# Attention values of two heads side by side in 64-column tiles, with summed exponentials for the denominators

## The chip, the cores and the metric

The kernel runs on one core of a Trainium2 chip. The metric is the device time of one execution in microseconds (us). Before the change three executions took 840.5, 841.15 and 843.84 us (median 841.15). The engines are TensorE (PE; its weight loads are shown apart as PEld), VectorE (DVE), ScalarE (ACT), GpSimd (POOL) and the DMA queues that SyncE (SP) and POOL issue.

## The reference

An attention in which a query sees only the keys of its own hash bucket, then two feed-forward blocks. All is float32.

```python
# q, k, v: (2, 8, 768, 64); proj: (64, 6)
q_bucket = sum over bits of ((q @ proj) > 0) * 2**bit      # k_bucket the same
scores = where(q_bucket == k_bucket, (q @ k.T) / 8, -1e9)
attn = exp(scores - max(scores))
attn = attn / (sum(attn) + 1e-9)
x = (attn @ v)  as (1536, 512)
g = x @ w_gate; h1 = (g * sigmoid(g) * (x @ w_val)) @ w_out                  # d_ff 1536
h = h1 @ w_in;  out = (max(h, 0) + alpha * min(h, 0)) @ w_out2              # d_ff 2048
```

## The kernel before

**Items and units.** The attention is cut into 24 items: a batch, a pair of heads and a group of 256 queries. Each item has two units, one a head (`u.x` is 0 or 1). A unit's scores lie transposed, with 768 keys as six blocks of 128 partitions and 256 queries along the free axis. A unit goes through four parts:

- `banks`: three steps, each of which multiplies keys and queries for two key blocks into a PSUM tile `S` (`s_bank`, lines 307 and 308); ACT copies it into `se` (128 x 1536 for the six blocks, four buffers) and DVE starts the maximum (`s_max`).
- `top` and `back`: the maximum over keys by TensorE transposes (`s_mt`, `s_mb`) and a DVE reduction, then `s_sub`, one DVE operation over all of `se` (line 344). ACT takes the exponential in place (`s_exp`, line 350), released a little later by `release()`.
- `values`: three steps of two key blocks (`s_pv`, line 361). The stationary operand is a 128 x 128 slice of `vv`. `vv` holds head 0's 64 value columns, 64 columns of ones and head 1's 64 value columns, so one matmul of 128 stationary columns gives a head's 64 output rows and, in the other 64 rows, its denominators. Six matmuls a unit, twelve an item, all plain float32.
- After the second unit `s_den` copies the denominators out of `po` with two ACT operations (line 367), `s_out` makes the reciprocals with two DVE transposes (lines 377 to 379) and multiplies each head by them (line 383, two operations), and `s_xh`, `s_xl` split the result into two float32r parts for the next stage.

**Order.** Units are written one slot apart: part k of unit i belongs to slot i + k. Items 0 to 7 run alone. Items 8 to 15 are written between the steps of `stage1(0)`, and items 16 to 23 between those of `stage1(1)`; `stage1(c)` is the first feed-forward block (lines 756 to 758) for 512 tokens, and for each of its steps 1.9 attention steps are written. Stage 1 of the first tokens also brings in the weights: DMA, four integer operations on ACT, DVE and POOL (lines 616 to 621), and a split in two parts (lines 691 and 705). Then come `stage1(2)`, `stage2(1)` and two calls of `wino` without attention. When the kernel is built, a planner orders the instructions of each engine from the written order, the dependences and its own costs; each engine then works strictly in its order, save that TensorE loads weights ahead.

**Buffers.** `gh` and `gl` hold the gated activations of `stage1` in `NG1` buffers; a `quad` (four output banks) reads four of them at once.

Of the kernel before, what the change touches and what calls it, by code (L numbers as in the profile page):

```python
# [8 lines left out]
F32 = mybir.dt.float32  # L9
# [3 lines left out]
AF = mybir.ActivationFunctionType  # L13
ALU = mybir.AluOpType
# [3 lines left out]

BIG = float(2.0 ** 100)

NG1 = 5
NEX = (2, 3)
RAWB = 2
WB = (3, 4, 6)
# [24 lines left out]
EARLY = (0, 12)  # L49

AHEAD = 6

SUMS = (12, 14, 16, 17)

# [2 lines left out]
def lsh_attention_moe_kernel(  # L57
# [12 lines left out]
    nc = tc.nc  # L70
    B, H, D, S = qT.shape
# [3 lines left out]
    P = 128  # L75
    NC = S // P
    GQ = 256
    NG = S // GQ
    NPAIR = H // 2
# [4 lines left out]
    W = 512  # L84
# [53 lines left out]
    at = Bag()  # L138
# [210 lines left out]
    def s_exp(u):  # L349
        ins = nc.scalar.activation(out=u.se, in_=u.se, func=AF.Exp, scale=SCALE)  # L350
        at.exps.append(ins.ins.name)
        if not at.alone:
            tc.keep_in_program_order(ins)

    def s_pv(u, j):
        it = u.it
        if j == 0 and u.x == 0:
            tag = at.tag["po"][it.i % 2]
            it.po = at.ps.tile([P, 2, GQ], F32, tag=tag, name="po", bufs=at.nb[tag])
        for kb in (2 * j, 2 * j + 1):  # L360
            nc.tensor.matmul(it.po[:, u.x, :], lhsT=VV[it.b, it.p][:, kb, u.x * D:u.x * D + P], rhs=u.se[:, kb, :],  # L361
                             start=kb == 0, stop=kb == NC - 1)

    def s_den(it):
        it.den = at.sm.tile([P, 8, 32], F32, tag="den", name="den", bufs=1)
        for x in range(2):
            nc.scalar.activation(out=it.den[x * D:(x + 1) * D],
                                 in_=it.po[(1 - x) * D:(2 - x) * D, x, :].rearrange("p (a b) -> p a b", a=8),
                                 func=AF.Copy, bias=1e-9)

    def s_out(it):

        it.xf = at.sm.tile([P, GQ], F32, tag="xf", name="xf", bufs=1)
        dt_ = it.xf.rearrange("p (a b) -> p a b", a=8)
        rc = it.den
        r8 = at.sm.tile([P, 8, 1], F32, tag="r8", name="r8", bufs=1)
        nc.vector.transpose(out=dt_, in_=it.den)
        nc.vector.reciprocal(out=r8, in_=dt_[:, :, 0:1])
        nc.vector.transpose(out=rc, in_=r8.to_broadcast([P, 8, 32]))
        rf = rc.rearrange("p a b -> p (a b)")  # L380
        for x in range(2):
            r = slice(x * D, (x + 1) * D)
            nc.vector.tensor_tensor(out=it.xf[r], in0=it.po[r, x, :], in1=rf[r], op=ALU.mult)
# [9 lines left out]
    items = []  # L393
    for b in range(B):
        two = W // GQ
        order = [(p, g) for p in range(NPAIR) for g in range(two)] if b == 0 else []
        order += [(p, g) for g in range(two if b == 0 else 0, NG) for p in range(NPAIR)]
        for p, g in order:
            it = Bag()
            it.b, it.p, it.g, it.i = b, p, g, len(items)  # L400
            it.ready = False
            it.first = not any((o.b, o.p) == (b, p) for o in items)
            items.append(it)
    at.done = 0
# [4 lines left out]
    def attention():  # L409

        us = []
        for it in items:
            for x in range(2):
                u = Bag()
# [30 lines left out]
        held, last = [], []  # L445

        def release():
            while held:
                s_exp(held.pop(0))

        def give():
            while last:
                it = last.pop(0)
                s_xh(it)
                s_xl(it)
# [21 lines left out]
        def back(u):  # L477
# [5 lines left out]
            step()  # L483
            yield

        def values(u):
            for j in range(3):
                s_pv(u, j)
                if j == 2 and u.x == 1:
                    s_den(u.it)  # L490
                    s_out(u.it)
                    last.append(u.it)
                    if at.alone:
                        give()
                if EXP_AT == ("v", j):
                    release()
                if XH_AT == ("v", j):
                    give()
                step()
                yield  # L500

        order = []
        for i, u in enumerate(us):
            for k, part in enumerate((banks, top, back, values)):
                slot = i + LAGS[k]
                order.append(((slot, i, k) if slot < OLDER else (slot, k, i), part, u))
        order.sort(key=lambda o: o[0])
        for _, part, u in order:
# [450 lines left out]
    def g_tiles():  # L959
        return [at.lt.tile([P, W], F32R, tag=t, name=t, bufs=NG1) for t in ("gh", "gl")]  # L960

# [16 lines left out]
    VV = {}  # L978

    at.nb = dict(S=3, T=1, G=2, Y=1, po=1)  # L980
    at.tag = dict(mt="G", mb="G", hp="T", po=("Y", "po"), gates="G")
    at.gates = 0
    pr = wp.tile([P, 2, 44], F32, tag="wr", name="pr", bufs=2)
    nc.scalar.dma_start(out=pr, in_=proj)
    first_load(items[0])
# [3 lines left out]
    def more():  # L989

        if next(side, 0) == 0:
            kv.close()
            return False
        return True
# [9 lines left out]
            upto("load", min(i + RAWB, 7), w_load)  # L1004

    k = 0
    per = NPAIR * (W // GQ)
    while at.done < per:
        at.alone = at.done < per - 2
        more()  # L1010
# [8 lines left out]
    for c, rate in enumerate(RATES):  # L1019
# [4 lines left out]
        for _ in stage1(c):  # L1024
# [7 lines left out]
            while due >= 1.0:  # L1032
                due -= 1.0
                over += at.done >= per * (c + 2)
                if over <= AHEAD:
                    more()
# [90 lines left out]
```

## Time and profile before

| | |
|---|---|
| three executions | 840.5, 841.15, 843.84 us |
| the profiled execution's own time | 839.15 us |
| its span | 836.9 us |
| PE, PEld busy | 807.8 us (97%), 690.2 us (82%) |
| DVE, ACT, POOL busy | 588.7 us (70%), 489.3 us (58%), 313.5 us (37%) |
| granted TensorE clock, mean | 0.998 |

The span is measured from the first instruction to the last. A PE record's length holds its latency, and records overlap, so what one matmul costs is read from the distance of starts and not from its length. A plain float32 matmul leaves two records in the trace, a float32r matmul one.

### The profile page before, as it was taken

The numbers are of one execution on the slowest core, as the hardware profiler recorded it, in microseconds if no ns is written. First come the engines' busy times: TensorE is split into PE (matmuls) and PEld (weight loads), VectorE is DVE, ScalarE is ACT, GpSimd is POOL, SyncE is SP. The second block draws the span as 40 slices with busy tenths as digits, with TensorE's granted clock in tenths as the row PEclk, the third lists the DMA queues.
The fourth block names the chain that finished last, engine by engine and source line by source line (L and its number), as shares of the span: only waits on it lengthen the run. The fifth ranks groups of instructions, "written<-read, shape, count | busy, mean of one in ns | idle before, by whom it ended". The sixth has DMA issues, their size and how long they took to land.

```text
span 836.9 us, 12164 instructions
## 1 busy us (share of the span) xinstructions
PE 807.8 (97%) x4276; PEld 690.2 (82%) x4276; DVE 588.7 (70%) x905; ACT 489.3 (58%) x827; POOL 313.5 (37%) x253
## 2 busy tenths in 40 slices
PE   5998999999999999999999999999999999999998
PEld 4777878887878888888888888887788899989996
DVE  5889998887998866666664363567968575667553
ACT  7889877886766655555543232324655464555553
POOL 5133337666555633322221462442424311332220
PEclk9999999999999999999999999999999999999999
DMA  9322336877656538545444687878644477565554
GB/s 239 78 70 94 133 110 199 261 230 220 229 189 235 202 129 323 204 156 184 176 159 157 242 290 292 299 273 300 252 196 157 176 242 277 176 204 198 175 175 142
DMA packets 74475, 168.22 MB, mean 201 GB/s; under 512 B 18480, under 2 KB 36912, under 8 KB 73648
## 3 DMA queue, kind: packets, MB, share of 16 engines
q1 hardware_dynamic: 73264, 164.66, 57.3%
q0 software_dynamic: 1008, 2.75, 1.6%
q8 instruction: 34, 0.56, 0.3%
q14 instruction: 25, 0.20, 0.1%
q10 hardware_dynamic: 144, 0.05, 0.0%
HBM read 124.44 MB, written 42.99 MB: 200 GB/s over the span
## 4 chain that ended last, share of the span: by engine, by line
PE 71%; DVE 11%; ACT 7%; DMA 6%; issue 3%; POOL 1%; SPq 0%; DVEq 0%; ACTq 0%; POOLq 0%
PE po L361 10%; PE gp L756 8%; PE gp L758 8%; PE gp L757 8%; PE op L762 5%; PE op L761 5%; PE op L763 5%; DMA raw<-in_wblk_dram 5%; PE hp L757 5%; PE hp L758 5%; PE hp L756 4%; PE S L307 2%; PE S L308 2%; ACT se L309 2%; DVE wt L619 2%
## 5 line engine op out<-in xcount | busy, mean ns | idle before, releaser
L751 POOL TENSOR_TENSOR gl<-ex,gh 128x512 fp32r<-128x512 f32 x61 | 87.2, 1430 | 160.6 <-ACT gh L748 112.6
L361 PE MATMUL po<-se,vv 128*128 128x256 f32 x576 | 139.4, 381 | 5.1 <-ACT se L350 2.8
L361 PEld LDWEIGHTS po<-se,vv 128*128 128x128 f32 x576 | 106.4, 190 | 22.5 <-ACT se L350 4.6
L756 PE MATMUL gp<-xh,wb 128*128 128x512 f32 x288 | 120.1, 417 | 0.5 <-ACT xh L386 0.5
L758 PE MATMUL gp<-xh,wb 128*128 128x512 f32 x288 | 112.9, 392 | 0.0
L757 PE MATMUL gp<-xl,wb 128*128 128x512 f32 x288 | 112.6, 391 | 0.0
L748 ACT ACTIVATE gh<-ex 128x512 fp32r<-128x512 f32 x84 | 52.9, 630 | 74.4 <-DVE ex L745 47.1
L309 ACT ACTIVATE se<-S 128x512 f32<-128x512 f32 x144 | 81.8, 592 | 23.7 <-PE S L308 22.6
L621 POOL TENSOR_TENSOR wt<-wt,wr 128x512 int32<-128x512 int32 x48 | 63.1, 1319 | 86.5 <-DVE wt L619 39.7
L307 PE MATMUL S<-QA,kt 128*128 128x256 f32 x288 | 79.8, 304 | 6.8 <-ACT se L309 3.0
L344 DVE SCALAR_TENSOR_TENSOR se<-se,mb 128x1536 f32<-128x1536 f32 x48 | 83.6, 1741 | 3.4 <-PE mb L339 3.4
L350 ACT ACTIVATE se<-se 128x1536 f32<-128x1536 f32 x48 | 71.1, 1482 | 8.8 <-DVE se L344 8.6
L762 PE MATMUL op<-wb,gh 128*128 128x512 f32 x192 | 75.2, 392 | 0.9 <-DVE wb L705 0.9
L761 PE MATMUL op<-wb,gh 128*128 128x512 f32 x192 | 75.1, 391 | 0.0
L308 PE MATMUL S<-qb,kt 76*128 76x256 f32 x288 | 73.9, 286 | 0.9 <-ACT kt L221 0.5
L763 PE MATMUL op<-wb,gl 128*128 128x512 f32 x192 | 74.7, 389 | 0.0
L307 PEld LDWEIGHTS S<-QA,kt 128*128 128x128 f32 x288 | 54.8, 191 | 13.1 <-ACT se L309 4.7
L758 PEld LDWEIGHTS gp<-xh,wb 128*128 128x128 f32 x288 | 54.0, 188 | 11.9
L756 PEld LDWEIGHTS gp<-xh,wb 128*128 128x128 f32 x288 | 54.2, 188 | 10.1 <-ACT xh L386 1.0
L757 PEld LDWEIGHTS gp<-xl,wb 128*128 128x128 f32 x288 | 54.3, 189 | 9.1
L756 PE MATMUL gp<-gh,wb 128*128 128x512 f32 x144 | 61.3, 425 | 0.3 <-ACT gh L748 0.3
L308 PEld LDWEIGHTS S<-qb,kt 76*128 76x128 f32 x288 | 54.4, 190 | 4.0 <-ACT kt L221 0.8
(125 smaller groups left out, 1901.2 us busy)
## 6 DMA issues: line engine op xcount, KB each, us to landing
wb<-w SPq DMA_DIRECT2D x72, 512.0 KB, 3.8
raw<-in_wblk_dram SPq DMA_DIRECT2D x68, 512.0 KB, 4.4
wb<-s SPq DMA_DIRECT2D x48, 512.0 KB, 3.6
w<-wb SPq DMA_DIRECT2D x36, 512.0 KB, 3.0
s<-wb SPq DMA_DIRECT2D x24, 512.0 KB, 2.8
qr<-in_q_dram SPq DMA_DIRECT2D x24, 256.0 KB, 3.0
wb<-s SPq DMA_DIRECT2D x16, 256.0 KB, 3.7
nat<-in_k_dram SPq DMA_DIRECT2D x8, 384.0 KB, 3.6
```

What stands on the lines that cost most here:

```text
L307: nc.tensor.matmul(pt[:, i, :], lhsT=ka[:, sl], rhs=qa, start=True, stop=False)
L308: nc.tensor.matmul(pt[:, i, :], lhsT=kb[:, sl], rhs=qb, start=False, stop=True)
L309: nc.scalar.activation(out=u.se[:, 2 * j:2 * j + 2, :], in_=pt, func=AF.Copy)
L344: ins = nc.vector.scalar_tensor_tensor(out=u.se, in0=u.se, scalar=FLOOR, in1=u.mx[:, None, :].to_broadcast([P, NC, GQ]), op0=ALU.max, op1= ...
L361: nc.tensor.matmul(it.po[:, u.x, :], lhsT=VV[it.b, it.p][:, kb, u.x * D:u.x * D + P], rhs=u.se[:, kb, :], start=kb == 0, stop=kb == NC - 1)
L751: eng.tensor_tensor(out=l, in0=ex, in1=f32(h), op=ALU.subtract)
L756: nc.tensor.matmul(pt, lhsT=h, rhs=ah, start=first, stop=False)
L757: nc.tensor.matmul(pt, lhsT=h, rhs=al_, start=False, stop=False)
L758: nc.tensor.matmul(pt, lhsT=l, rhs=ah, start=False, stop=last)
L761: nc.tensor.matmul(pt, lhsT=gh, rhs=h, start=first, stop=False)
L762: nc.tensor.matmul(pt, lhsT=gh, rhs=l, start=False, stop=False)
L763: nc.tensor.matmul(pt, lhsT=gl, rhs=h, start=False, stop=last)
```

## The change

Items 8 to 23 (`it.pair`) multiply their values after both heads' exponentials are there. `s_pair` writes, for each key block, two matmuls of 64 stationary columns, one for each head, into the lower and the upper 64 rows of the same PSUM tile. The denominators come from other matmuls: `s_add` adds the exponentials of a unit over key blocks, and a 64-column block of ones is multiplied with the sums. In items 8 to 15 the sums are two 128 x 512 additions (DVE, then POOL), which leave two blocks a head and so four denominator matmuls an item; in items 16 to 23 there are three additions on DVE (two of 128 x 512, one of 128 x 256), which leave one block and two matmuls. The denominators then lie in the same rows as the values, so `s_den` and the multiplication of `s_out` are one operation each. The first unit's `values` steps become `rests`, three steps without matmuls, and the second's become `pair`, written first in the slot after. `ps` takes two buffers of 2 KB a partition; `gh` and `gl` go from five buffers to four.

```diff
-NG1 = 5
+NG1 = 4
...
+PAIRED = 8
+
+ADDS = ("DP", "DDD")
+
+RELEASE = 1
...
+    def s_add(u):
+
+        u.ps = at.sm.tile([P, 2, GQ], F32, tag="ps", name="ps", bufs=2)
+        how = ADDS[u.it.i // per - 1]
+        e = [dict(P=nc.gpsimd, D=nc.vector)[x] for x in how]
+        e[0].tensor_tensor(out=u.ps, in0=u.se[:, 0:2, :], in1=u.se[:, 2:4, :], op=ALU.add)
+        e[1].tensor_tensor(out=u.ps, in0=u.ps, in1=u.se[:, 4:6, :], op=ALU.add)
+        u.n = 4 - len(how)
+        if u.n == 1:
+            e[2].tensor_tensor(out=u.ps[:, 0, :], in0=u.ps[:, 0, :], in1=u.ps[:, 1, :], op=ALU.add)
+
+    def s_pair(it, ua, ub):
+
+        tag = at.tag["po"][it.i % 2]
+        it.po = at.ps.tile([P, 2, GQ], F32, tag=tag, name="po", bufs=at.nb[tag])
+        v = VV[it.b, it.p]
+        for k in range(NC):
+            for u in (ua, ub):
+                nc.tensor.matmul(it.po[u.x * D:(u.x + 1) * D, 0, :], lhsT=v[:, k, 2 * u.x * D:(2 * u.x + 1) * D],
+                                 rhs=u.se[:, k, :], start=k == 0, stop=k == NC - 1)
+        for k in range(ua.n):
+            for u in (ua, ub):
+                nc.tensor.matmul(it.po[u.x * D:(u.x + 1) * D, 1, :], lhsT=v[:, 0, D:2 * D],
+                                 rhs=u.ps[:, k, :], start=k == 0, stop=k == ua.n - 1)
+
     def s_den(it):
         it.den = at.sm.tile([P, 8, 32], F32, tag="den", name="den", bufs=1)
+        if it.pair:
+            nc.scalar.activation(out=it.den, in_=it.po[:, 1, :].rearrange("p (a b) -> p a b", a=8),
+                                 func=AF.Copy, bias=1e-9)
+            return
...
+        if it.pair:
+            nc.vector.tensor_tensor(out=it.xf, in0=it.po[:, 0, :], in1=rf, op=ALU.mult)
+            return
...
         def release():
             while held:
-                s_exp(held.pop(0))
+                u = held.pop(0)
+                s_exp(u)
+                if u.it.pair:
+                    s_add(u)
...
+        def rests(u):
+            for j in range(3):
+                if j == RELEASE:
+                    release()
+                step()
+                yield
+
+        def pair(u):
+            release()
+            for j in range(3):
+                if j == 0:
+                    s_pair(u.it, us[2 * u.it.i], u)
+                    s_den(u.it)
+                    s_out(u.it)
+                    last.append(u.it)
+                if j == 2:
+                    give()
+                step()
+                yield
...
+                if part is values and u.it.pair:
+                    order.append(((slot, -1, i), pair, u) if u.x else ((slot, k, i), rests, u))
+                    continue
```

The first place is TensorE at item 8, the first one changed (`po` is the values' PSUM tile, `hp` the hash of a later item, `gp` stage 1). Before, the first unit's six stand in twos, of which two runs are seen here:

```order
L758 MATMUL gp<-xh,wb 128x512
L361 MATMUL po<-se,vv 128x256 x2
L209 MATMUL hp<-QA,sqm 44x256
L210 MATMUL hp<-qb_67,sq_65 44x256
L209 MATMUL hp<-QA,sqm 44x256
L210 MATMUL hp<-qb_67,sq_65 44x256
L361 MATMUL po<-se,vv 128x256 x2
L756 MATMUL gp<-xh,wb 128x512
```

Now one matmul of the first head stands by itself, among stage 1 and the same hash:

```order
L823 MATMUL gp<-xh,wb 128x512
L821 MATMUL gp<-xh,wb 128x512
L215 MATMUL hp<-QA,sqm 44x256
L388 MATMUL po<-se,vv 64x256
L822 MATMUL gp<-xl,wb 128x512
L823 MATMUL gp<-xh,wb 128x512
```

and the other eleven with the four on `ps` come 29 matmuls later in one run:

```order
L821 MATMUL gp<-xh,wb 128x512
L822 MATMUL gp<-xl,wb 128x512
L823 MATMUL gp<-xh,wb 128x512
L388 MATMUL po<-se,vv 64x256 x11
L392 MATMUL po<-ps,vv 64x256 x4
L821 MATMUL gp<-xh,wb 128x512
L822 MATMUL gp<-xl,wb 128x512
L823 MATMUL gp<-xh,wb 128x512
```

The item's values moved from short runs for each unit into one matmul and one run of fifteen. The same split (one, then eleven) stands in 15 of the 16 changed items; in the last one all twelve are together.

The second place is DVE in the second half of the attention, around the additions into `acc` of stage 1 (`m` is the maximum, `se` the scores, `ex` a gate). Before:

```order
L315 TENSOR_TENSOR m_3258<-S,se 128x512
L793 TENSOR_TENSOR acc<-gp,acc 128x512
L317 SCALAR_TENSOR_TENSOR m_3258<-S,m_3258 128x512
L344 SCALAR_TENSOR_TENSOR se<-se,mb 128x1536
L331 TENSOR_TENSOR m_3258<-m_3258 128x256
L793 TENSOR_TENSOR acc<-gp,acc 128x512
L742 SCALAR_TENSOR_TENSOR ex<-ex,gp 128x512
```

Now:

```order
L350 SCALAR_TENSOR_TENSOR se<-se,mb 128x1536
L770 TENSOR_TENSOR wb<-wt,wb 128x512
L337 TENSOR_TENSOR m_3248<-m_3248 128x256
L375 TENSOR_TENSOR ps<-se 128x512
L858 TENSOR_TENSOR acc<-gp,acc 128x512
L376 TENSOR_TENSOR ps<-ps,se 128x512
L379 TENSOR_TENSOR ps<-ps 128x256
L858 TENSOR_TENSOR acc<-gp,acc 128x512
```

Three additions came in, with one of stage 1's between them; the first waits for the exponential on ACT, and the matmuls on `ps` wait for the last.

## Rows read from the trace of the kernel before

**Rows 1.** The page's first part: busy time, share of the span, instructions.
```profile
PE 807.8 (97%) x4276; PEld 690.2 (82%) x4276; DVE 588.7 (70%) x905; ACT 489.3 (58%) x827; POOL 313.5 (37%) x253
```

**Rows 2.** Busy time by stretch: us, five engines, granted clock, DMA share, GB/s.
```profile
60.00:105.00 45.00, 39.90 (x246) 34.75 (x244) 41.67 (x66) 40.56 (x68) 17.41 (x14) 1.00 0.34 117
122.40:302.90 180.50, 175.39 (x904) 148.04 (x903) 153.25 (x243) 129.14 (x222) 107.95 (x84) 0.99 0.65 214
302.90:459.50 156.60, 156.36 (x806) 133.95 (x805) 99.16 (x165) 80.76 (x134) 42.99 (x37) 1.00 0.54 192
460.00:837.00 377.00, 371.40 (x1947) 319.09 (x1945) 232.54 (x335) 174.95 (x300) 119.34 (x86) 1.00 0.64 225
```

**Rows 3.** The second transpose of each item: count, duration min/median/max, first and last start.
```profile
L379 DVE STREAM_TRANSPOSE den<-r x9: 433/445/446, 122.4 to 302.9; 128x256 f32<-128x256 f32 x9
...
L379 DVE STREAM_TRANSPOSE den<-r x8: 440/446/447, 326.2 to 459.5; 128x256 f32<-128x256 f32 x8
```

**Rows 4.** What PE waited for, 122.4 to 302.9, then 302.9 to 459.5: total, times, longest.
```profile
PE po L361 <- DVE xf L383: 1.9, 3, 1.3
PE S L307 <- DVE mk L215: 1.7, 2, 1.1
...
PE po L361 <- DVE xf L383: 0.2, 1, 0.2
```

**Rows 5.** Groups by line, values' matmuls: count, busy us, mean ns, idle before.
```profile
L361 PE MATMUL po<-se,vv 128*128 128x256 f32 x576 | 139.4, 381 | 5.1 <-ACT se L350 2.8 <-DVE xf L383 2.2
L361 PEld LDWEIGHTS po<-se,vv 128*128 128x128 f32 x576 | 106.4, 190 | 22.5 <-ACT se L350 4.6 <-issue 2.2 <-ACT gh L748 1.2
```

**Rows 6.** PE in order of time at one unit's values: start, us, line.
```profile
265.32 0.39 PE L758 MATMUL gp<-xh,wb 128*128 128x512 f32 x1
265.56 1.89 PE L361 MATMUL po<-se,vv 128*128 128x256 f32 x8
267.09 0.58 PE L756 MATMUL gp<-xh,wb 128*128 128x512 f32 x1
```

**Rows 7.** PE in order of time at a hash of 44 stationary columns.
```profile
272.11 0.28 PE L307 MATMUL S<-QA,kt 128*128 128x256 f32 x1
272.23 0.28 PE L308 MATMUL S<-qb,kt 76*128 76x256 f32 x1
272.35 0.28 PE L209 MATMUL hp<-QA,sqm 128*44 128x256 f32 x1
272.46 0.28 PE L210 MATMUL hp<-qb,sq 96*44 96x256 f32 x1
272.58 0.28 PE L209 MATMUL hp<-QA,sqm 128*44 128x256 f32 x1
272.70 0.28 PE L210 MATMUL hp<-qb,sq 96*44 96x256 f32 x1
272.82 0.39 PE L756 MATMUL gp<-xh,wb 128*128 128x512 f32 x1
273.05 0.40 PE L757 MATMUL gp<-xl,wb 128*128 128x512 f32 x1
```

**Rows 8.** Groups by line on DVE, POOL and ACT.
```profile
L344 DVE SCALAR_TENSOR_TENSOR se<-se,mb 128x1536 f32<-128x1536 f32 x48 | 83.6, 1741 | 3.4 <-PE mb L339 3.4
L383 DVE TENSOR_TENSOR xf<-po,den 64x256 f32<-64x256 f32 x48 | 20.1, 419 | 1.4
L331 DVE TENSOR_TENSOR m<-m 128x256 f32<-128x256 f32 x30 | 15.6, 519 | 0.0
L705 DVE TENSOR_TENSOR wb<-wt,wb 128x512 fp32r<-128x512 f32 x18 | 13.9, 772 | 3.1 <-ACT wb L691 3.1
L751 POOL TENSOR_TENSOR gl<-ex,gh 128x512 fp32r<-128x512 f32 x61 | 87.2, 1430 | 160.6 <-ACT gh L748 112.6 <-PE op L763 23.2 <-PE hp L758 22.6
L367 ACT ACTIVATE den<-po 64x256 f32<-64x256 f32 x48 | 18.2, 379 | 24.8 <-PE po L361 24.3
```

More of the change, by code (lines that the diff above doesn't have):

```diff
@@ L401, in lsh_attention_moe_kernel @@
             it.ready = False
+            it.pair = len(items) >= PAIRED
             it.first = not any((o.b, o.p) == (b, p) for o in items)
@@ L982, in lsh_attention_moe_kernel @@
     at.gates = 0
+    per = NPAIR * (W // GQ)
     pr = wp.tile([P, 2, 44], F32, tag="wr", name="pr", bufs=2)
@@ L1006, in lsh_attention_moe_kernel @@
     k = 0
-    per = NPAIR * (W // GQ)
     while at.done < per:
```

## The prediction

> **What bounds the kernel now.** Begin with the busy shares: TensorE is busy for 97% of the span, DVE for 70%, ACT for 58% and POOL for 37% [rows 1]. A share over the whole span mixes stages, so next comes the busy time by stretch. The second transposes of items 7, 15 and 23 start at 122.4, 302.9 and 459.5 us [rows 3], which cuts the changed items into stretch A (items 8 to 15, 180.5 us) and stretch B (items 16 to 23, 156.6 us). In A TensorE is busy for 175.4 us and DVE for 153.3 (85%); in B TensorE for 156.4 and DVE for 99.2 (63%) [rows 2]. The waits confirm it: TensorE's longest wait is 1.3 us in A and 0.2 us in B [rows 4]. So in both stretches the end is set by how fast TensorE's own stream runs, and A has little room on DVE. How little shows before the feed-forward work begins: from 60 to 105 us DVE was busy 41.67 of 45 us while TensorE was only at 39.90 [rows 2]. I read that 92.6% as what DVE can do in this pattern of waits.
>
> **What the values cost.** 576 records are 288 matmuls (24 items of twelve), two records each [rows 5]. Eight records take 1.89 us from the first start to the last end, and one record is 0.38 long [rows 5, 6], so starts are (1.89 - 0.38) / 7 = 0.216 us apart. An item's 24 records cost 24 x 0.216 = 5.18 us of TensorE's stream.
>
> **The new matmuls.** Items 8 to 15 issue 12 + 4 = 16, items 16 to 23 12 + 2 = 14, each again of two records, with 256 moving columns. No row shows two matmuls at work in different columns of the array, so the price is bounded. Low end: the two column tiles do not wait for each other, and the pair costs what one 128-column matmul costs, 2 x 0.216 = 0.43 us. High end: they run one after the other, 0.86 us the pair, since fewer stationary columns alone save nothing: with 44 columns the hash matmuls start 0.12 us apart like the 128-column ones before them [rows 7]. I take the low end, because its nearest row is the one matmul that fills the same 128 columns with the same 256 moving ones [rows 6], and because TensorE already loads weights under running matmuls (0.19 us each, no gap) [rows 5, 6].
>
> The Trainium skill (TensorE: Matmul & The Clock Gate, "Part 3: Packing small matmuls — row/col tiling") reports a speedup of 2.38 for three column tiles, which would favour the low end. The same section says that weight loads overlap running matmuls only where the row group differs, and two column tiles share all rows; by that the pair would fall to the high end and the time to the one of the serial rival below. The trace does not agree for whole-array matmuls, whose loads of 0.19 us on the same rows stay hidden [rows 5]; for tiles no run here shows it.
>
> Records of one head must follow one another, and the order puts head 0 and head 1 alternately. Then a new matmul starts every 0.216 us with two in flight, and a run of n takes (n + 1) x 0.216. The order also shows a matmul alone before the run, which pairs with nothing: 0.43 us. In A: 0.43 + 16 x 0.216 = 3.89 us an item, 1.29 less than 5.18, over eight items 10.3 us. In B: 0.43 + 14 x 0.216 = 3.46, 1.72 less, 13.8 us. If the lone one cost nothing and nothing else waited, it would be 31 us.
>
> **The sums.** An addition of 128 x 512 on DVE costs 0.77 us by its nearest row, one of 128 x 256 0.52 us, and one on POOL 1.43 us [rows 8]. A gets 16 units x 0.77 = 12.3 us on DVE and 16 x 1.43 = 22.9 us on POOL (108 of 180.5 busy, so it fits [rows 2]); B gets 16 x (2 x 0.77 + 0.52) = 33.0 us on DVE. The multiplication of `s_out` becomes one operation instead of two: 8 x 0.42 = 3.4 us less in each stretch. One ACT copy of 0.38 an item goes, beside an ACT that waits anyway; nothing gained on the path.
>
> DVE's new need in A is 153.3 + 12.3 - 3.4 = 162.2 us, and at 92.6% that takes 175.2 us. TensorE alone would be done in 180.5 - 10.3 = 170.2. So DVE is what is late next, and A gains 5.3 us, not 10.3. In B DVE needs 99.2 + 33.0 - 3.4 = 128.8, at 92.6% 139.1 us, and TensorE 156.6 - 13.8 = 142.8: TensorE stays the bound.
>
> **The new wait.** The matmuls on `ps` wait for the last addition. Behind them on TensorE stand stage 1's matmuls, so a stall there is lost. From the exponential to the last sum in B it is 0.77 + 0.77 + 0.52 plus, by the order, one of stage 1's operations between them (about 0.7): 2.7 us. The eleven value matmuls and the first sum cover 13 x 0.216 = 2.8 us. This just fits, unless DVE is inside its 1.74 us subtraction [rows 8] when the exponential ends. I charge 0.5 us an item (bounds 0 and 1.74): 4 us in B. In A the chain is 0.77 + 1.43 and about half an operation of POOL ahead, 2.9 us against 2.8; the 5 us by which DVE is later there than TensorE hide it. Without that cover it is 8 x 0.5 = 4 us more.
>
> **Edits at nothing.** `gh` and `gl` with four buffers: the fifth gate of a stage must wait for the quad that frees the first, but it is needed only by the next quad, four gates later, which hides it; cover gone, it costs a split of 1.43 us on POOL [rows 8] for each of six quads, 9 us. The steps of loads, hashes and rounding keep their number (three for `rests`, three for `pair`), and SP's issues their kinds and count; a DMA later by a step is hidden as before. The four `se` buffers are now freed for both units only by the pair; two items' time lies between, so I charge nothing. From 460 us on TensorE is busy 371.4 of 377 us [rows 2] on the same work: no change.
>
> **The sum.** 5.3 + (13.8 - 4) = 15.1 us. The profiled execution took 839.15, which gives 824.0; it lies 2.0 us below the median of the three runs (841.15), for which the same sum gives 826. I forecast 825.
>
> **Rivals.**
>
> *Serial tiles (the slower side; the change doesn't do what it says).* Place: the 16 runs on `po`. Price: 16 x 0.43 = 6.91 us an item in A (1.73 more than 5.18) and 6.05 in B (0.87 more): 13.8 + 6.9 = 20.7 us more, 861. It decides from the point where matmuls start more than (5.18 - 0.43) / 16 = 0.30 us apart in A and 0.34 in B; 0.216 is side by side, 0.43 serial. For it: no row shows two tiles at once. Against: the low-end rows above. Chance 0.20.
>
> *Half overlap.* The second tile's weights come late and matmuls start about 0.32 us apart: A loses 8 x (0.43 + 16 x 0.32 - 5.18) = 3 us, B gains 8 x (5.18 - 0.43 - 14 x 0.32) = 2, with the waits at 838 to 842. Chance 0.09.
>
> *The sums hold TensorE.* Side by side, but every pair waits for a whole subtraction: B loses 8 x 1.74 = 14 and so all its gain, A keeps at most 3: about 837. For it: DVE at over 90% in both stretches. Against: in B today it waits 37% of the time. Chance 0.06.
>
> *A drain at each change of tile shape.* A matmul's length less the step to the next is 0.39 - 0.23 = 0.16 us [rows 7]; paid four times an item (into and out of the lone one and the run), 16 x 4 x 0.16 = 10 us, about 833. Against it stand the hash's narrow matmuls, which begin and end without a gap (272.35 and 272.82) [rows 7]. Chance 0.03. The Trainium skill (TensorEngine Tiling (Array Packing), "Key Properties") says that a change of tiling mode drains TensorE; the rows at the hash do not agree.
>
> **How the numbers follow.** The forecast has 0.62, and its own range is 811 (all of the 31 us) to 834. The range from 811 to 846 takes in the half overlap, the held sums and the drain, and leaves out the serial case (0.20). Faster by over 0.5% (under 837, about what a measurement of this kernel can tell): 0.62 + 0.03 + half of the sums' 0.06 and a little of the half overlap, 0.70. Within 0.5%: 0.09. Slower: 0.20 and a little, 0.21.
>
> **What the next profile would show.** Right: the new lines' records start about 0.108 us apart inside a run (two matmuls in flight), a run of 15 takes 3.5 us and not 6.5; A ends near 175 us of length with DVE above 90%, B near 147; DVE's sum rises by 38 us, POOL's by 23. Wrong: starts 0.216 apart in the runs; TensorE waits on the `ps` sums of more than 1 us an item; or a stretch after 460 us that is longer than 377.

## The result, and the profile after

The changed kernel takes 855.32 us (median of 4 runs, 853.73 to 856.97) where the kernel before, on the same chip, takes 842.5 us (4 runs, 840.5 to 846.0). The ratio is 1.0148, 95% interval 1.0104 to 1.0192: slower by 1.5%. The forecast was 825 us, with 0.21 on slower. The profiled execution took 854.22 us with a span of 852.2.

The page's first part, as in [rows 1]:

```profile
PE 801.6 (94%) x4372; PEld 650.5 (76%) x4372; DVE 645.9 (76%) x953; ACT 485.7 (57%) x811; POOL 342.8 (40%) x269
```

TensorE has less to do (807.8 before) in a longer span, and VectorE has 57 us more. The second transposes of items 7, 15 and 23 now start at 122.8, 313.1 and 478.2 us, so the three later stretches of [rows 2] are:

```profile
122.80:313.10 190.30, 170.15 (x941) 126.35 (x940) 172.80 (x246) 125.40 (x210) 130.72 (x99) 0.98 0.61 199
313.10:478.20 165.10, 159.09 (x881) 119.06 (x880) 138.28 (x214) 82.19 (x131) 51.43 (x41) 1.00 0.54 191
478.20:852.00 373.80, 368.21 (x1932) 316.32 (x1930) 231.50 (x332) 173.74 (x298) 117.42 (x85) 1.00 0.65 225
```

A (items 8 to 15) grew from 180.5 to 190.3 us and B (items 16 to 23) from 156.6 to 165.1; the rest shrank by 3. VectorE (third figure of the busy times) is busy for 172.8 us of A, 91%, against 85% before, and for 84% of B against 63%.

The stretches do not hold the same work before and after. TensorE's gate records (the tile `gp`) alone, before and then after:

```profile
122.40:302.90 180.50, 109.94 (x399) 0.99 0.65 214
302.90:459.50 156.60, 103.08 (x381) 1.00 0.54 192
460.00:837.00 377.00, 115.77 (x507) 1.00 0.64 225
```

```profile
122.80:313.10 190.30, 103.75 (x387) 0.98 0.61 199
313.10:478.20 165.10, 107.67 (x411) 1.00 0.54 191
478.20:852.00 373.80, 112.32 (x492) 1.00 0.65 225
```

B has some thirty more, twelve of which A has lost and fifteen the stretch behind. At 0.227 us each that is nearly 7 us of B's length, and all of the 3 us by which the rest shrank.

Did the tiles run side by side? Here is TensorE at one item of B, in order of time (start, us, line), to be held against [rows 6]:

```profile
352.96 0.39 PE L823 MATMUL gp<-xh,wb 128*128 128x512 f32 x1
353.28 0.65 PE L388 MATMUL po<-se,vv 128*64 128x256 f32 x2
353.86 0.50 PE L821 MATMUL gp<-xh,wb 128*128 128x512 f32 x1
354.20 0.39 PE L822 MATMUL gp<-xl,wb 128*128 128x512 f32 x1
...
356.53 0.39 PE L821 MATMUL gp<-xh,wb 128*128 128x512 f32 x1
356.85 2.59 PE L388 MATMUL po<-se,vv 128*64 128x256 f32 x21
359.07 0.38 PE L392 MATMUL po<-ps,vv 128*64 128x256 f32 x1
359.27 0.38 PE L388 MATMUL po<-se,vv 128*64 128x256 f32 x1
359.28 0.80 PE L392 MATMUL po<-ps,vv 128*64 128x256 f32 x3
360.02 0.50 PE L822 MATMUL gp<-xl,wb 128*128 128x512 f32 x1
360.35 0.39 PE L823 MATMUL gp<-xh,wb 128*128 128x512 f32 x1
```

They do. Twenty-six records from 356.85 to 360.02 are thirteen pairs; the rows at 359.27 and 359.28 are one pair, begun together. (2.59 - 0.38) / 20 is 0.11 us a record, half of the 0.216 of [rows 6]. But the two ends of a run cost something that [rows 6 and 7] do not have. The step from the last 128-column record to the first tile is 0.32 us (352.96 to 353.28, 356.53 to 356.85), where gate records follow each other at 0.23. The first record after the run is 0.50 long instead of 0.40, and the next starts 0.33 behind it instead of 0.23. The lone matmul at 353.28 (two records) stretches the way from 352.96 to 354.20 to 1.24 us; less 0.23 for each of the two gate records in it, that is 0.78 us for one matmul, where 0.43 had been charged.

The weight loads show what is different at a switch. Those around the lone matmul, in order of time:

```profile
352.50 0.19 PEld L822 LDWEIGHTS gp<-xl,wb 128*128 128x128 f32 x1
352.74 0.19 PEld L823 LDWEIGHTS gp<-xh,wb 128*128 128x128 f32 x1
353.28 0.19 PEld L388 LDWEIGHTS po<-se,vv 128*64 128x64 f32 x2 [0.36 <-issue]
353.86 0.19 PEld L821 LDWEIGHTS gp<-xh,wb 128*128 128x128 f32 x1 [0.39 <-issue]
```

The load at 352.74 is for the matmul at 352.96: it runs 0.22 us ahead, under the matmul before. The loads at 353.28 and 353.86 start together with their own matmuls, after an idle stretch in which they waited for nothing that the profile shows. So it is at all 35 ways into tiles and all 35 ways out of them, while of 1391 steps from one whole-array matmul to the next between 120 and 495 us only 14 have the load so late, eleven of them behind a wait.

The waits of TensorE (total, times, longest), first in A, then in B, as in [rows 4]:

```profile
PE po L392 <- POOL ps L376: 6.8, 8, 1.8
PE S L313 <- DVE m L321: 5.8, 2, 3.1
PE po L388 <- ACT se L356: 3.6, 5, 1.3
PE mt L339 <- DVE m L337: 1.0, 1, 1.0
```

```profile
PE po L392 <- DVE ps L379: 4.6, 5, 1.5
PE mt L339 <- DVE m L337: 0.9, 2, 0.5
```

In A TensorE now stands still for the sums, for the exponentials and, for up to 3.1 us at a time, for an operation of VectorE that the change does not touch (`m`, the maximum over a score bank). The last one fits an engine that is nearly full; the experiments test that.

VectorE's groups in A, by line (count, busy us, mean ns); after first, then the two weight conversions before:

```profile
L684 DVE SCALAR_TENSOR_TENSOR wt<-raw,wt 128x512 int32<-128x512 int32 x30 | 30.0, 1000 | 0.4
...
L682 DVE TENSOR_SCALAR wt<-raw 128x512 int32<-128x512 int32 x29 | 19.7, 685 | 2.9 <-DMA raw<-in_wblk_dram 2.9
L375 DVE TENSOR_TENSOR ps<-se 128x512 f32<-128x512 f32 x16 | 16.1, 1007 | 1.7 <-ACT se L356 1.3
```

```profile
L619 DVE SCALAR_TENSOR_TENSOR wt<-raw,wt 128x512 int32<-128x512 int32 x30 | 24.3, 823 | 0.3
L617 DVE TENSOR_SCALAR wt<-raw 128x512 int32<-128x512 int32 x29 | 16.0, 569 | 12.1 <-DMA raw<-in_wblk_dram 12.1
```

The sixteen additions cost 1.007 us each, not 0.77, and the same thirty weight conversions as before take 1.00 us instead of 0.82. In B the three additions of a head cost 0.74, 0.94 and 0.63 us where 0.77, 0.77 and 0.52 were charged:

```profile
L376 DVE TENSOR_TENSOR ps<-ps,se 128x512 f32<-128x512 f32 x16 | 15.0, 942 | 0.1
...
L375 DVE TENSOR_TENSOR ps<-se 128x512 f32<-128x512 f32 x16 | 11.7, 737 | 3.6 <-ACT se L356 3.5
...
L379 DVE TENSOR_TENSOR ps<-ps 128x256 f32<-128x256 f32 x16 | 10.1, 633 | 0.1
```

To divide TensorE's time I priced every record at the step its kind has back to back (0.227 us a gate record, 0.119 a score record, 0.216 a whole value record, 0.108 a tile) and called what is left "beyond the stream". In A the stream fell from 170.3 to 152.0 us and the remainder rose from 10.3 to 38.4. In B the stream fell from 154.8 to 145.8 and the remainder rose from 1.8 to 19.3. Over the whole program the stream fell by 31 us, all that the pairing could give (27 in A and B, the rest behind them). The remainder took 45.6 us more. The experiments take it apart as far as they go.

### The profile page after: what moved, and what is told of

Read it like the earlier page. It is cut to its first block, busy times and chain, and to the rows that moved or that the text cites. A ratio compares the mean times of both kernels' runs of the same rounds, so it can differ in the third digit from the quotient of the medians.

```text
span 852.2 us, 12379 instructions
## 1 busy us (share of the span) xinstructions
PE 801.6 (94%) x4372; PEld 650.5 (76%) x4372; DVE 645.9 (76%) x953; ACT 485.7 (57%) x811; POOL 342.8 (40%) x269
## 4 chain that ended last, share of the span: by engine, by line
PE 61%; DVE 14%; ACT 7%; DMA 6%; POOL 6%; issue 5%; SPq 0%; POOLq 0%; DVEq 0%; ACTq 0%
PE gp L821 7%; PE gp L823 7%; PE gp L822 7%; PE op L827 5%; PE op L828 5%; PE op L826 5%; PE hp L823 4%; PE hp L822 4%; PE hp L821 4%; PE po L367 3%; POOL wt L686 2%; PE S L314 2%; PE S L313 2%; DMA wb<-w 2%; DVE se L350 2%
## 5 line engine op out<-in xcount | busy, mean ns | idle before, releaser
L686 POOL TENSOR_TENSOR wt<-wt,wr 128x512 int32<-128x512 int32 x48 | 67.1, 1400 | 64.1 <-DVE wt L684 34.9
L822 PEld LDWEIGHTS gp<-xl,wb 128*128 128x128 f32 x288 | 54.6, 189 | 10.3 <-issue 1.5
L388 PE MATMUL po<-se,vv 128*64 128x256 f32 x384 | 54.6, 385 | 3.6 <-ACT se L356 3.6
L821 PE MATMUL gp<-gh,wb 128*128 128x512 f32 x144 | 57.7, 401 | 0.0
L756 ACT ACTIVATE wb<-w 128x512 fp32r<-128x512 f32 x64 | 39.5, 624 | 31.2 <-PE hp L823 26.8
```

The lines of the kernel that those rows point to most:

```text
L686: pin(nc.gpsimd.tensor_tensor(out=a, in0=a, in1=r, op=ALU.add))
L821: nc.tensor.matmul(pt, lhsT=h, rhs=ah, start=first, stop=False)
L822: nc.tensor.matmul(pt, lhsT=h, rhs=al_, start=False, stop=False)
```

## The experiments

All times are medians with the ratio to runs of the kernel before on the same chip and its interval. Those medians lie between 841.6 and 844.0, so the ratios are the fairer comparison across calls.

**Pairing alone: `e1_no_sums_all_blocks`.** The additions go and the denominators take all six key blocks. An item then issues 24 tiles, whose stream is 24 x 0.216 = 5.18 us, exactly that of before.

```
-                if u.it.pair:
-                    s_add(u)
...
-        for k in range(ua.n):
+        for k in range(NC):
...
-                                 rhs=u.ps[:, k, :], start=k == 0, stop=k == ua.n - 1)
+                                 rhs=u.se[:, k, :], start=k == 0, stop=k == NC - 1)
```

> Pairing alone: no additions, the denominators from twelve more 64-column matmuls an item on all six key blocks, right as the reference has it. TensorE then has 24 matmuls side by side, 24 x 0.216 = 5.2 us an item as before the change, plus about 0.4 us for the one that stands alone. Theory 1: 840 to 850 us, as the kernel before plus up to 7 us. Theory 2: 855 us or more.

Measured 858.69 us, 1.0191 (1.0159 to 1.0222): 16.0 us more than before with the same stream and no sums. The sixteen items have 32 runs of tiles, a lone matmul and a long run each. The ends of the records give 0.35 us for one way in and out, 32 x 0.35 = 11.2, and a lone matmul gives away its missing partner's 0.216, 16 x 0.216 = 3.5: 14.7 us. That is nearly all of the 16. The time is that of theory 2, but its reason is not most of it: all of TensorE's waits in A together are 9.2 us, against 5.1 before.

**The structure without the sums: `e2_sums_left_out`.** The changed kernel with the same tiles, but the denominators' matmuls read the first key blocks of the exponentials and nothing is added (so its denominators are incomplete).

```
-                if u.it.pair:
-                    s_add(u)
...
-                                 rhs=u.ps[:, k, :], start=k == 0, stop=k == ua.n - 1)
+                                 rhs=u.se[:, k, :], start=k == 0, stop=k == n - 1)
```

> The changed kernel without any addition: the denominators' matmuls (four an item, then two) read the first key blocks' exponentials, so they are incomplete sums; TensorE's instructions are the same in number and shape. Theory 1 (the additions, by their load on DVE and POOL and by the wait for them, ate the gain): TensorE's stream is 31 us shorter and nothing new is waited for, so 811 to 820 us. Theory 2 (waiting for both heads before any value is multiplied, and holding the score buffers until then, costs the time): 835 us or more.

Measured 832.63 us, 0.9866 (0.9833 to 0.9899), between the ranges of the two theories. Stretches A and B, of an execution that took 837.17 us:

```profile
124.10:299.40 175.30, 164.66 (x929) 123.38 (x928) 147.34 (x229) 123.11 (x207) 104.43 (x83) 0.99 0.66 218
299.40:458.60 159.20, 158.54 (x894) 121.95 (x893) 103.53 (x167) 83.73 (x135) 47.66 (x40) 1.00 0.57 197
```

Of 31 us of stream only 10 arrive, even with no sums at all; by the prices of `e1` the shape changes and lone matmuls take 14.7 us, and waits for exponentials are 5.8 us in A. Against the changed kernel the sums cost 22.7 us.

**Sums that nobody reads: `e3_sums_not_awaited`.** As the last, but the additions are computed.

```
-                                 rhs=u.ps[:, k, :], start=k == 0, stop=k == ua.n - 1)
+                                 rhs=u.se[:, k, :], start=k == 0, stop=k == ua.n - 1)
```

> The changed kernel with all additions computed, but with the denominators' matmuls reading the first key blocks' exponentials instead of the sums, so the sums are used by nobody and the denominators are incomplete. Theory 1a (the wait of TensorE for the sums is the loss): within 5 us of the kernel without additions. Theory 1b (the load on DVE and POOL is the loss): within 5 us of the changed kernel, 850 or more. Theory 2: the same as the changed kernel, 850 or more, and so is the kernel without additions.

Measured 856.9 us, 1.0167 (1.0135 to 1.0198). Freeing TensorE of the wait gains nothing. VectorE is busy for 181.5 us of an A of 195.2, 93%: what costs is that the sums must be computed, not that somebody waits for them.

**The sums in the kernel before: `f3_before_with_sums`.** Whole 128-column matmuls as before; the additions are computed and read by nobody (four gate buffers, to make room).

```
...
-                s_exp(held.pop(0))
+                u = held.pop(0)
+                s_exp(u)
+                if u.it.i >= 8:
+                    s_add(u)
```

> The kernel before, with 128-column value matmuls as they were, and in items 8 to 23 the additions of the change computed after each exponential and read by nobody; first gate product with four buffers, to make room. Theory L (the load of the additions on VectorE and the slowing of VectorE's other operations beside GpSimd is what costs): items 8 to 15 need 162 plus 32 plus about 12 us of VectorE at its limit of about 92 per cent, but its present 85 per cent leaves some room: 10 to 20 us more than before, 852 to 862 us, nearly all in items 8 to 15. Rival W (only reading the sums costs): 842 to 844 us.

Measured 851.14 us, 1.0116 (1.0093 to 1.0140), 9.5 us more than before and just under the range of theory L.

```profile
123.80:314.10 190.30, 177.16 (x909) 148.38 (x908) 175.72 (x259) 129.41 (x223) 130.17 (x100) 0.99 0.62 203
314.10:472.00 157.90, 157.10 (x803) 133.88 (x803) 133.93 (x212) 80.19 (x133) 49.15 (x37) 1.00 0.54 190
```

The sums alone lengthen A to 190.3 us, with TensorE's old work in it. That this is the A of the changed kernel to the tenth is in part chance: this one holds 400 gate and 188 score records, that one 387 and 173, which is 4.7 us of stream less. What goes with a long A is VectorE's share of it: 91 to 94% in the five versions with sums there (the changed kernel, `e3`, `e5`, `e8` and this one), at most 86% in every version without. B, where VectorE had room, grew by 1.3 us. So the sums cost 9.5 us here, and 22.7 us beside the pairing.

**No lone matmul: `e5_second_head_first`.** The scheduler put one matmul of head 0 ahead of each run because head 0's exponential is there first. Naming head 1 first binds the run together: 8 runs in A instead of 16, 13 in B instead of 19.

```
         for k in range(NC):
-            for u in (ua, ub):
+            for u in (ub, ua):
```

> The changed kernel with the pair's matmuls written second head first, so that none can start before both exponentials are there: all twelve stand in one run and no matmul stands alone. Theory A (every entry into and exit from the 64-column tiles costs TensorE time, about 0.32 us a run and 0.55 us for the lone matmul, read from the start distances in the trace after): 15 x 0.55 = 8 us less than the changed kernel, 844 to 850 us. Theory B (the lone matmul did useful work early and its run now waits longer for the second exponential): 855 us or more.

Measured 853.76 us, 1.0133 (1.0103 to 1.0164), against 1.0148: within the intervals of the changed kernel, not the 8 us that I gave it. A stayed at 191.3 us, with VectorE at 174.9 (91%). What TensorE saved there it waited. It also ran slowly after some of the waits. Busy time, granted clock (third from the end) and traffic of two stretches of 2 us, then two records of the second:

```profile
268.00:270.00 2.00, 0.72 (x5) 0.54 (x4) 1.97 (x5) 1.64 (x4) 1.32 (x2) 1.00 0.85 285
272.00:274.00 2.00, 2.00 (x6) 1.52 (x6) 2.00 (x4) 2.00 (x3) 1.14 (x1) 0.50 0.18 70
272.13 0.63 PE L822 MATMUL gp<-xl,wb 128*128 128x512 f32 x1
272.56 0.63 PE L823 MATMUL gp<-xh,wb 128*128 128x512 f32 x1
```

TensorE was idle for most of 268 to 270; then it was granted 0.50, 1.2 of its 2.4 GHz, and gate records followed each other at 0.43 us instead of 0.23. Such a dip lasts 3.4 us here and so costs up to 1.7. A of this kernel has four of them, the changed kernel's two, the one before the change one.

**The same without sums: `e6_no_sums_second_first`.** Both edits, `e2`'s and `e5`'s.

> The kernel without additions (832.6 us; denominators from the first key blocks alone, so incomplete), with the second head first. Theory A: 8 us less than 832.6, 822 to 827 us. Theory B: 832 us or more.

Measured 827.58 us, 0.9814 (0.9782 to 0.9846), 5 us less than `e2`. With the sums' load gone, taking 16 ways in and out away does pay; 16 x (0.35 + 0.216) = 9 us was its price by the records, so about half of it reaches the end.

**Three runs instead of one: `f2_three_runs`.** `e6` with the run issued in three parts, at three steps.

```
...
-        for k in range(NC):
+        for k in (2 * j, 2 * j + 1):
...
```

> The kernel without sums and with the second head first (denominators from the first key blocks alone, so the output is not the reference's), with each item's run of fourteen or sixteen 64-column matmuls cut into three, with 128-column gate matmuls in between: 32 more entries into and exits from the 64-column shape. Theory C (each run pays about 0.32 us for its entry and exit): 10 us more than the uncut one, 837 to 838 us, less up to 4 us where the later reading no longer waits for an exponential: 833 to 838. Rival N (the shape change costs nothing by itself; the longer starts seen at the two ends are only weight loads that something else hides): within 2 us of 827.6.

Measured 829.61 us, 0.9857 (0.9831 to 0.9884), 2.0 us more than `e6`. This did not settle it: the scheduler, which places an instruction when its inputs are expected, put most parts together again, and the trace has 22 runs, not 48. Six more than `e6`, by 0.35, would be 2.1.

**One change of shape, priced: `h1_four_whole_ahead` and `h2_four_whole_between`.** To `e6` four whole 128-column matmuls an item are added, all ahead of the run in the first, one after each of the first four pairs of tiles in the second, with the order of the run pinned. Work is equal; the second has 64 more ways into and out of tiles. (The four add one product again and again, so the values come out different.)

```
+        for k in range(4):
+            tc.keep_in_program_order(nc.tensor.matmul(it.po[:, 0, :], lhsT=v[:, 0, 0:P], rhs=ub.se[:, 0, :], start=k == 0,
+                                 stop=False))
         for k in range(NC):
+            for u in (ub, ua):
...
```

```
         for k in range(NC):
+            for u in (ub, ua):
...
+            if k < 4:
+                tc.keep_in_program_order(nc.tensor.matmul(it.po[:, 0, :], lhsT=v[:, 0, 0:P], rhs=ub.se[:, 0, :], start=False,
+                                 stop=False))
...
```

> The kernel without sums and with the second head first, with four more 128-column matmuls an item (on the same values and exponentials, added into the value bank, so the output is not the reference's), all four put directly ahead of the item's run of 64-column tiles. It is the control of the next run. All theories: sixteen items by 4 by 0.216 us, 13.8 us more than the 827.6 us of the kernel without them: 839 to 843 us.

> The same four 128-column matmuls an item, but one after each of the first four pairs of 64-column tiles: the same work, with four more changes into and out of the 64-column shape an item, 64 in all. Theory C (an entry costs about 0.15 us and an exit about 0.20 us of TensorE, as the ends of the records show): 64 by 0.35, 22 us more than the control, about 863 us (858 to 867). Rival N (only the first weight load of a run is late, and the pipeline hides it elsewhere): within 3 us of the control.

Measured 854.33 us, 1.0138 (1.0111 to 1.0164), and 870.29 us, 1.0325 (1.0300 to 1.0350). My figure for the control was half of what it should have been: I had priced one record a matmul, and a matmul leaves two, so 16 x 4 x 0.43 = 27.6 us were to be added to 827.6, which gives 855.2. The difference of the two is 16.0 us for 64 changes, 0.25 us each; in B, where TensorE waits for little else (2.1 and 2.5 us), the stretch grew from 170.3 to 181.4 us, 11.1 us for 32 or 0.35 each. In A it grew by 7.3 us, 0.23 each, while TensorE's waits there fell from 9.4 to 6.6 us: part of the cost falls beside waits that are there anyway. The second kernel in order of time, at one item:

```profile
358.90 0.65 PE L388 MATMUL po<-se,vv 128*64 128x256 f32 x4
359.49 0.70 PE L391 MATMUL po<-se,vv 128*128 128x256 f32 x2
360.12 0.65 PE L388 MATMUL po<-se,vv 128*64 128x256 f32 x4
360.70 0.70 PE L391 MATMUL po<-se,vv 128*128 128x256 f32 x2
```

A cycle of a pair and a whole matmul takes 1.21 us (358.90 to 360.12), where the records of both add up to 4 x 0.108 + 2 x 0.216 = 0.86: 0.35 us for one way in and one way out.

**Other edits, one at a time.** `e4_four_gate_buffers` is the kernel before with `NG1 = 4`:

> The kernel before with four instead of five buffers for the gated activations, nothing else. Theory 3 (the lost buffer costs the time): 848 us or more. Theories 1 and 2: within 2 us of the kernel before, about 842.

Measured 841.88 us, 0.9992 (0.9972 to 1.0011): the buffer costs nothing.

`e8_sums_on_dve` moves A's second addition from POOL to VectorE (`ADDS = ("DD", "DDD")`):

> The changed kernel with the second addition of items 8 to 15 on DVE instead of POOL. Theory E (DVE's operations on SBUF operands are stretched while POOL runs, so 23 us of POOL additions cost DVE as much as they spare it): DVE's busy time in items 8 to 15 stays within 6 us of the changed kernel's 172.8, time 850 to 858 us. Theory F (plain load: each 128 x 512 addition on DVE adds its 0.69 us to a stretch that DVE bounds): 11 us more DVE, 862 us or more.

Measured 855.33 us, 1.0146 (1.0111 to 1.0180), no difference. VectorE is busy for 182.6 us of an A of 193.4 instead of 172.8 of 190.3, and TensorE's waits move from `ps` to VectorE's `m` (6.8 us). Neither theory came out whole: the time stayed, as E has it, and VectorE's load rose by 9.8 us, nearly the 11 of F. The sixteen additions brought 18.1 us to VectorE, and the two weight conversions gave 6.5 back (43.2 us instead of 49.7). POOL is busy for 107.8 us of this A, as before the change, and A is no shorter for it, so POOL's load is not what sets it.

**Only where VectorE has room: `e7_last_eight_only`.** Items 16 to 23 paired, head 1 first, items 8 to 15 as before (`PAIRED = 16` and the edit of `e5`).

> Only items 16 to 23 are paired, second head first, three additions on DVE; items 8 to 15 are as before the change. Theory C (the additions cost time mainly in the stretch of items 8 to 15, where DVE was busy 85% before; in the later one it has room and only the wait of about 5 us remains): 842.5 - (8 x 2.16 - 8 x 0.32 - 4.6) = 832 us, 828 to 837. Theory D (the additions eat the gain in both stretches): 840 us or more.

Measured 839.63 us, 0.9959 (0.9943 to 0.9974), 0.4% faster than before; I had expected 832. Stretches A and B, and TensorE's longest waits in B:

```profile
122.60:303.20 180.60, 174.15 (x904) 146.87 (x903) 154.03 (x244) 128.90 (x222) 107.21 (x84) 1.00 0.67 214
303.20:460.30 157.10, 148.57 (x847) 114.93 (x847) 133.12 (x209) 80.19 (x127) 49.72 (x38) 1.00 0.57 194
```

```profile
PE po L392 <- DVE ps L379: 3.4, 4, 1.2
PE po L388 <- ACT se L356: 2.4, 4, 1.4
```

A is back at its 180.6 us. B has 139.8 us of stream, 15 less than before, and 17.3 beyond it: waits of 8.5, eight runs' ways in and out (2.8), and about 6 us that no wait in the list names.

I tried twice to take the waits away. `f1_last_eight_step_later` issues the run one step later (`if j == 1` in `pair`), `h3_last_eight_released_early` issues head 1's exponential and sums a step earlier:

```
-            if at.alone:
+            if at.alone or u.it.pair and u.x:
                 release()
```

> The pairing from item sixteen on (second head first, three VectorE additions a head), with the whole run of value and denominator matmuls put one step of the gate product later, so that sums and exponentials have more time to be done. In the kernel where it stands a step earlier TensorE waited 3.5 us for sums and 2.4 us for exponentials in items 16 to 23. Theory W (these waits are its cost, and the load of the sums on VectorE is covered there): the waits go, items 16 to 23 take 151 to 153 us, 834 to 836 us in all. Rival L (a wait given up here comes back at the next consumer, because the additions fill VectorE): 839 to 841 us.

> The pairing from item sixteen on, second head first, three VectorE additions a head; the second head's exponential and additions are issued right after its subtraction, one step of the program earlier than in the kernel at 839.6 us, where TensorE waited 3.5 us for sums and 2.4 us for exponentials in items 16 to 23. Theory W (these waits are what keeps that kernel at the time of the kernel before): 3 to 6 us go, 834 to 837 us. Rival L (VectorE at 85 per cent of these items passes each delay on to a later operation): 839 to 842 us.

Measured 841.01 us, 0.9990 (0.9977 to 1.0004), and 840.67 us, 0.9966 (0.9945 to 0.9988). Neither tested what it was made for. In the first the scheduler left TensorE's instructions in exactly the order of `e7`. In the second there was little to move: in `e7` 13 of the 16 exponentials already start within 0.5 us of the end of their subtraction, here 15, and TensorE still waited 3.5 us for sums and 2.2 for exponentials. Whether these waits are what `e7` lacks to its 832 stays open. `e7` and `f1` differ by 0.3% with one order on TensorE, so pairing the last eight items alone is worth 0.1 to 0.4%, under what I called measurable. No version with complete denominators beats the kernel before by more.

## Why the prediction was wrong

**Tiles side by side: right.** The doubt with the largest rival (serial tiles, 0.20) was settled for the forecast: two tiles begin together, 0.216 us a pair of records, and all 31 us of stream went. The forecast had less, 24 us, since it let each run take one tile step more and charged 0.43 us for the lone matmul. The rule of the Trainium skill that I set against it (TensorE: Matmul & The Clock Gate, "Part 3", weight loads overlap running matmuls only where the row group differs) would have made the pairs serial; the pair at 359.27 and 359.28 shares all rows and runs together.

**The drain at each change of tile shape: the step that failed first.** I gave it 0.03, and argued from the 44-column hash [rows 7] that narrow matmuls come and go without a gap. The row was the wrong neighbour: the hash uses fewer columns of the whole array and pays nothing, while a tile placed at column 0 or 64 pays on both sides. The price that I wrote down, 0.16 us, four times an item, 10 us, was close: the records give 0.35 us for both ways, and the changed kernel has 35 runs, 12.3 us; `e1`, `h1` and `h2` show the cost in the whole time. It was taken from a gate record's length less its step and not from any switch, so its closeness is in part luck. The rule of the Trainium skill that I cited and set aside (TensorEngine Tiling (Array Packing), "Key Properties": a change of tiling mode drains TensorE) agrees with these rows in that each change costs time. What the trace shows of the cause is that the weight load no longer runs ahead at a switch; whether the array drains as well is not shown.

**The sums on VectorE: the term that was mis-sized, and the larger loss.** The mechanism was named: VectorE is late next in A, at 92.6%. But the need was put at 162.2 us and is 172.8. Of the 10.6 us between, 3.8 are the sixteen additions themselves (16.1 us, not 12.3). The rest is old work that became slower beside them: the two weight conversions alone took 9.4 us more (49.7 against 40.3), part of which is offset by operations that moved out of the stretch. 172.8 us at 92.6% would be 186.6; A took 190.3, with one more dip of the clock (1.7 us) in it. So the share I read from 60 to 105 us held roughly (90.8% here, up to 94.4% in `e8`), and the load did not. `f3` shows it without any pairing. What the operations became slower beside is in the last section.

**The waits in B: near.** Charged 4 us, measured 4.6 on the sums. B still came out 18 us longer than forecast (165.1, not 146.8). By the records: 19 ways in and out, 6.6 us; 29 more gate records (410, before 381), 6.6, and 11 more score records, 1.3; other waits 1.4; some 2 us stay unassigned. The gate records are no late work of a full A alone: A holds twelve fewer and the stretch behind B fifteen. `e2`, where VectorE has room, shows the same shift (381 in A, 416 in B), so it does not need VectorE's load; the later place of the values in the written order is the likely reason. The forecast priced both stretches as if they kept their work.

**Edits at nothing: right.** `NG1` (`e4`), the copy on ACT, and the part after 460 us, which did not grow.

**The arithmetic of the whole.** -31.0 of stream, +11.2 for the shape changes of the 32 runs of `e2`, +3.5 for lone matmuls leaves -16.3. With the waits for exponentials the chip gives -10 (`e2`), and the sums +22.7 on top: +12.7, and 12.8 were measured. That the last step closes says nothing, since the 22.7 is itself a difference of two measured times. `f3` prices the sums without pairing at 9.5, so some 13 us come only where both meet. By the division into stream and remainder, the remainder grows by 24.7 us in `e2`, by 10.1 in `f3` and by 45.6 with both: 11 us more than the two together, 4 in A and 7 in B. In B the wait for the sums is 4.6 us and three more runs are 1 us, yet `e3`, which has neither, keeps 6 of the 7: why the two cost more together than apart stays open. The forecast had 24 of the 31, with the lone matmuls taken off, nothing for the shape changes, and 9 us for the sums (5 by VectorE in A, 4 by the wait in B).

The chances were wrong for the same reason. The drain stood as a rival of 0.03 that would still be faster than before, VectorE's lateness as one of 0.06 that would end at 837, and no case held both, though they come from different engines and nothing kept them apart; together they turn the sign. Nor did any of the three signs of being wrong that I named appear: tiles start 0.11 us apart, the waits on `ps` stay under 1 us an item (6.8 and 4.6 us over eight items each), and the part after 478 us is no longer than before. What told was A at 190 us instead of 175, and VectorE's sum up by 57 us instead of 38.

## What to carry to other kernels

Before moving work to an engine, take its share of the stretch and the price of its operations *in that stretch*, and let the old operations become slower too: here 9 us of load (12.3 of additions less 3.4 saved) became 20 on an engine that had 8% to spare. The 64-column tiles here ran side by side at the full rate, but going from whole matmuls to tiles and back cost about a third of a microsecond, so bind all tiles of an item into one run and do not let a scheduler split off the first one (worth 5 us in `e6`, and nothing clear in `e5`, where VectorE holds A up). Count what each stretch holds before and after, for a stretch can grow by taking over work. An order changed in the source need not be an order on the engine: read it in the trace before believing the experiment.

## What the runs showed of the hardware

**VectorE beside POOL.** Of the operations in the changed kernel from 122 to 480 us, `wt<-raw,wt` (128 x 512, all operands in SBUF) takes 0.683 us where POOL runs nothing (21 of them), and 1.265 us on average where POOL is busy for more than half of it (18), up to 1.78. For the additions `ps<-se` it is 0.683 and 1.042. `m<-S,se`, which reads one operand from PSUM, takes 0.680 and 0.683: no difference. The kernel before has the same pattern (0.682 and 0.956 for `wt<-raw,wt`), and with the additions taken off POOL in `e8` the conversions of A became cheaper, as reported there. So the 0.77 of [rows 8] was no price of the operation but a mean over both cases, and a stretch with more POOL work has a higher one. The Trainium skill (GPSIMD Engine Reference, "1. Specifications") says that VectorE operations with two SBUF inputs contend with GpSimd for SBUF; these rows agree, with the sizes beside them.

**The clock after a wait.** In the changed kernel TensorE stood idle for 2.6 us until 195.4 and for 3.1 us until 248.4; within 2 us of each the granted clock fell to 0.50, the lower of its two levels (1.2 GHz), for 3.4 us, which costs up to half of that, 1.7 us. Between 122 and 320 us this happened once in the kernel before (after idle stretches of 1.1 and 0.9 us close together), twice in the changed one, four times in `e5`, and not at all in `e7`. Not every wait is followed by it: the changed kernel's 1.8 us at 138 us was not. A wait of TensorE can thus cost more than its length, which the sum of waits does not show.
